# A transform and a mixture of experts in one kernel: stage one beside the making of the matrices, turned matrices by products, and stages and logits that lag

## Chip, cores, metric

One core of one Trainium2 chip. The metric is the device time of one execution in microseconds (us), median of several. Runs here fell on several chips, and the same kernel takes 13 to 14% longer on some than on another, so times are compared on one chip only, and across chips by their ratio to the kernel before on the same chip.

## The reference

Eight images of 2496 rows and 256 channels. Each is filtered in the frequency domain, then every row goes to the one expert of eight that a gate with a bias per modality picks.

```python
def _attn_ref(x, filt_r, filt_i):                      # x (8, 2496, 256)
    X = np.fft.rfft(x, axis=1)
    Y = X * (filt_r + 1j * filt_i)[None, :, :]
    return np.fft.irfft(Y, n=x.shape[1], axis=1).astype(np.float32)

def _moe_ref(x, modality_id, w_gate, modality_bias, w1, w2):   # x (19968, 256), 8 experts, F 1024
    logits = x @ w_gate + modality_bias[modality_id]
    e_idx = np.argmax(logits, axis=1)
    # ... gate_w: softmax probability of the chosen expert
    for e in range(E):
        mask = e_idx == e
        h = np.maximum(x[mask] @ w1[e], 0.0)
        out[mask] = gate_w[mask, None] * (h @ w2[e])
```

## The kernel before

The transform is done by products in three stages. Stage one (L392) multiplies x with `w1m` and writes its result to memory (`b1_d`). Stage two reads it back with other rows on the partitions (`t2`), multiplies with `w2m` (L411), with the filters, and with the turned matrices `a1m` and `a2m` (L418, L419), and writes (`b2_d`). Stage three reads that back (`t4`) and multiplies with `wbm` (L462, L463); its rows `yo` are transposed (L472) and multiplied with the gate (L477). Then the image is routed, its rows are scattered into bins, and blocks of 256 rows of one expert go through two products (L645, L657). All matrices are made on the chip.

One pass of the inner loop is called a slot: a piece of every stage and 2.25 steps of expert work (a quarter of a block's products each).

```python
    bp = ctx.enter_context(tc.tile_pool(name="fbig", bufs=3))      # t2 and t4 together
    # ...  a1m, a2m: transpose w2m, then scatter the columns while copying out of PSUM
        for src, dst in ((w2m, a1m), (w2x, a2m)):
            for s0 in range(0, NS, SPB):
                tp = tpp.tile([KB, SPB, P], BF16, tag="tp")
                for i in range(SPB):
                    nc.tensor.transpose(tp[:, i, :KB], src[:, s0 + i, :], ident[:KB, :KB])
                nc.vector.tensor_copy(
                    dst[:, s0:s0 + SPB, :].rearrange("p s (jr t) -> p s t jr", jr=4),
                    tp[:, :, :KB].rearrange("p s (t jr) -> p s t jr", jr=4))
    # ...
    def stage2(g, k):
        s = k * EV
        if s < NS:
            if s % SCH == 0:                                       # load and use in one slot
                # ...
                nc.sync.dma_start(st[g]["t2"], src[:, s:s + SCH, :])
    # ...  stage3: the previous piece is transposed, copied and multiplied in one slot
            nc.tensor.transpose(pT[:, i, dc, :], yo[:, ub + i, dc * P:(dc + 1) * P], ident)
            # ...
            nc.vector.tensor_copy(yT, pT)
            # ...
            nc.tensor.matmul(psL[:, i, :], lhsT=yT[:, i, dc, :], rhs=wg[:, dc, :], ...)
    # ...  the main loop
    for i in range(B + 4):
        for k in range(NP + 1):                                    # 14 slots to an image
            if i < B and k < NP:
                stage1(i, k)
            if 0 <= i - 1 < B and k <= NS // EV:
                stage2(i - 1, k)
            if 0 <= i - 2 < B and k <= NPY:
                stage3(i - 2, k)
            # ...  scatter to bins, padding
            if 0 <= i - 2 < B and k == NPY + 1:
                route(i - 2)
                # ...
            owed += STEPS                                          # 2.25
            while owed >= 1:
                owed -= 1
                moe.step()
```

## Time and profile before

| | before |
|---|---|
| time, median of 3 | 946.2 us (942.0 to 947.9) |
| span of the profiled run | 935.8 us |
| first stage-one, stage-two, stage-three product | 43.5, 72.1, 127.1 us |
| last stage-three product | 712.2 us |
| from there to the end | 223.6 us |

The page's first part, busy us and share of the span by engine, shows that no engine is full:

```profile
PE 654.5 (70%) x4886; PEld 491.7 (53%) x4886; DVE 410.6 (44%) x1249; ACT 385.0 (41%) x689; POOL 375.6 (40%) x423
```

So the time is read by stretches, not by engines. The five times in the table are seams: start, filling of the three stages, steady work, and the expert work that is left. How each stretch looked before is shown in the prediction.

### The profile page before, as it was taken

The numbers are of one execution on the slowest core, as the hardware profiler recorded it, in microseconds if no ns is written. First come the engines' busy times: TensorE is split into PE (matmuls) and PEld (weight loads), VectorE is DVE, ScalarE is ACT, GpSimd is POOL, SyncE is SP. The second block draws the span as 40 slices with busy tenths as digits, with TensorE's granted clock in tenths as the row PEclk, the third lists the DMA queues.
The fourth block names the chain that finished last, engine by engine and source line by source line (L and its number), as shares of the span: only waits on it lengthen the run. The fifth ranks groups of instructions, "written<-read, shape, count | busy, mean of one in ns | idle before, by whom it ended". The sixth has DMA issues, their size and how long they took to land.

```text
span 935.8 us, 15940 instructions
## 1 busy us (share of the span) xinstructions
PE 654.5 (70%) x4886; PEld 491.7 (53%) x4886; DVE 410.6 (44%) x1249; ACT 385.0 (41%) x689; POOL 375.6 (40%) x423
## 2 busy tenths in 40 slices
PE   0316359459359776858877786779588449999996
PEld 0205236336236554645664565557356338878775
DVE  8812124424524543643472345447335324444442
ACT  1024334335235443634553463436133225555553
POOL 7032100450540543354444335343553664444545
PEclk9999999999656887978996898789788789999999
DMA  9299974644635742564563435232322323323320
GB/s 142 40 194 209 212 145 114 142 117 99 154 95 128 162 118 80 121 168 112 135 157 101 123 101 142 83 106 71 117 67 64 98 90 98 102 88 103 92 75 1
DMA packets 94347, 106.80 MB, mean 114 GB/s; under 512 B 13163, under 2 KB 77457, under 8 KB 94163
## 3 DMA queue, kind: packets, MB, share of 16 engines
q0 software_dynamic: 31008, 52.03, 25.1%
q1 hardware_dynamic: 63258, 53.75, 22.7%
q8 instruction: 44, 0.72, 0.3%
q14 instruction: 37, 0.29, 0.1%
HBM read 74.43 MB, written 54.31 MB: 138 GB/s over the span
## 4 chain that ended last, share of the span: by engine, by line
PE 55%; DMA 10%; issue 10%; another core or an unknown queue 9%; DVE 9%; ACT 6%; POOL 0%; DVEq 0%; POOLq 0%; SPq 0%; ACTq 0%
PE hps L645 16%; PE ops L657 16%; DMA b_d<-t 5%; PE ps L463 4%; PE ps L462 4%; PE lt L472 3%; DMA t<-b_d 3%; ACT t L395 3%; PE pz L418 3%; PE pz L419 2%; PE ps L392 2%; PE pT L634 2%; PE ps L411 2%; ACT hT L649 2%
## 5 line engine op out<-in xcount | busy, mean ns | idle before, releaser
L649 ACT ACTIVATE hT<-hps 128x512 f16<-128x512 f32 x340 | 198.6, 597 | 279.1 <-PE hps L645 139.6
L667 POOL DMA_INDIRECT out_dram<-osb,meta x170 | 167.7, 987 | 272.8 <-DVE osb L664 223.5
L645 PE MATMUL hps<-xT,w 128*128 128x256 f16 x1360 | 232.5, 291 | 32.8 <-issue 17.9
L657 PE MATMUL ops<-w2sb,hT 128*128 x1360 | 228.4, 288 | 10.8 <-issue 9.6
L534 POOL DMA_INDIRECT bins_d<-yo,pos_i x160 | 156.7, 979 | 50.9 <-issue 48.6
L645 PEld LDWEIGHTS <-w 128*128 128x128 f16 x1360 | 131.1, 103 | 62.4 <-issue 40.0
L657 PEld LDWEIGHTS <-hT 128*128 128x128 f16 x1360 | 138.6, 103 | 45.2 <-issue 19.1
L395 ACT CAST t<-ps 96x512 f16<-96x512 f32 x104 | 59.7, 582 | 125.5 <-PE ps L392 54.8
L425 DVE TENSOR_TENSOR p<-xf,g 104x512 f16<-104x512 f16 x96 | 40.7, 424 | 144.1 <-ACT xf L423 135.5
L411 PE MATMUL ps<-t,w2m 104*104 104x256 f16 x192 | 49.0, 348 | 78.4 <-DMA t<-b_d 54.3
L137 POOL DMA_DIRECT2D xt<-in_x_dram x32 | 17.6, 549 | 214.6 <-PE ps L392 175.7
L624 DVE COPY w<-w1sb 128x2048 f16 x85 | 59.2, 697 | 65.8 <-PE ops L657 40.9
L462 PE MATMUL ps<-t,wbm 96*96 96x256 f16 x160 | 58.7, 367 | 36.0 <-ACT t L395 17.9
L664 DVE TENSOR_SCALAR osb<-ops,meta 128x256 f32<-128x256 f32 x170 | 75.3, 477 | 16.3 <-PE ops L657 6.0
L418 PE MATMUL pz<-p,a1m 104*104 104x256 f16 x192 | 61.3, 334 | 23.4 <-DVE p L425 7.0
L423 ACT CAST xf<-ps 104x512 f16<-104x512 f32 x96 | 56.3, 588 | 51.1 <-PE ps L411 40.3
L411 PEld LDWEIGHTS <-w2m 104*104 104x104 f16 x192 | 29.6, 164 | 83.5 <-DMA t<-b_d 55.6
L432 ACT CAST z<-pz 104x512 f16<-104x512 f32 x96 | 56.6, 590 | 38.3 <-PE pz L419 13.5
L635 DVE COPY xT<-pT 128x512 f16<-128x512 f16 x85 | 35.8, 421 | 79.6 <-PE pT L634 36.2
L392 PE MATMUL ps<-xt,w1m 96*96 96x256 f16 x208 | 53.5, 356 | 16.2 <-ACT t L395 15.9
L419 PE MATMUL pz<-xf,a2m 104*104 104x256 f16 x192 | 62.5, 340 | 0.3
L474 DVE COPY yT<-lt 128x512 f16<-128x512 f16 x80 | 33.7, 421 | 62.4 <-PE lt L472 45.8
(188 smaller groups left out, 667.7 us busy)
## 6 DMA issues: line engine op xcount, KB each, us to landing
xs<-bins_d SPq DMA_DIRECT2D x85, 130.0 KB
t<-b_d SPq DMA_DIRECT2D x24, 416.0 KB
b_d<-z SPq DMA_DIRECT2D x48, 208.0 KB
xt<-in_x_dram POOLq DMA_DIRECT2D x24, 384.0 KB
b_d<-t SPq DMA_DIRECT2D x48, 192.0 KB
t<-b_d SPq DMA_DIRECT2D x24, 384.0 KB
w1sb<-in_moe_w_dram POOLq DMA_DIRECT2D x8, 512.0 KB
w2sb<-in_moe_w_dram POOLq DMA_DIRECT2D x8, 512.0 KB
```

What stands on the lines that cost most here:

```text
L392: nc.tensor.matmul(ps[:KA, i, :], lhsT=w1m, rhs=xt[:, t - t0 + i, :], start=True, stop=True)
L395: nc.scalar.copy(st[g]["t1"][:, k % 2], ps[:KA])
L411: nc.tensor.matmul(ps[:KB, i, :], lhsT=w2m[:, s + i, :], rhs=st[g]["t2"][:, s % SCH + i, :], start=True, stop=True)
L418: nc.tensor.matmul(pz[:KB, i, :], lhsT=a1m[:, s_ + i, :], rhs=p1[:, i, :], start=True, stop=False)
L419: nc.tensor.matmul(pz[:KB, i, :], lhsT=a2m[:, s_ + i, :], rhs=p2[:, i, :], start=False, stop=True)
L462: nc.tensor.matmul(ps[:KA, i, :], lhsT=wbm, rhs=t4[:, t - t0, :], start=True, stop=True)
L534: ins = nc.gpsimd.indirect_dma_start(out=bins_d[:, :], out_offset=IOA(ap=st[g]["pos"][:rows, t:t + 1], axis=0), in_=st[g]["yw"][:rows, t, ...
L645: mm = nc.tensor.matmul(hps[:, k, :], lhsT=b["w1"][:, dc, ft * P:(ft + 1) * P], rhs=b["xT"][:, dc].rearrange("p i t -> p (i t)"), start=(d ...
L649: nc.scalar.activation(b["hT"][:, q * FQ:(q + 1) * FQ, :], hps, AF.Relu)
L657: nc.tensor.matmul(b["ops"][:, i, :], lhsT=b["hT"][:, ft, i * P:(i + 1) * P], rhs=w2sb[:, ds(b["ej"], 1), ft, :], start=(ft == 0 and i == ...
L664: nc.vector.tensor_scalar_mul(osb[:, i, :], b["ops"][:, i, :], gate[:, i, :])
L667: ins = nc.gpsimd.indirect_dma_start(out=out[:, :], out_offset=IOA(ap=b["meta"][:, i, 0:1], axis=0), in_=osb[:, i, :], in_offset=None, **kw)
```

## The change

Four parts, meant to shorten the start and to keep PE fed in the middle.

1. *Start.* Stage one of the first image is issued as soon as `w1m` exists; the other matrices come after it in the program. The turned matrices are made by a product with a permuted identity, so that the copies out of PSUM are contiguous and can be split between DVE and ACT. Two smaller things ride along: the filters are read from memory once and copied, not read twice, and the experts' weights are asked for from the first slot of the loop on.
2. *Slots between stages and loads ahead.* Three slots lie between the end of one stage of an image and the start of the next, where there was one; the loads of `t2` and `t4` are issued two slots before their use. Their three shared buffers stay three.
3. *Logits.* A piece's transposition comes one slot after it, its gate products two slots after.
4. *Routing* is split in two slots (count, place) and comes later.

The diff, cut to its core (the moved lines that make room for it are left out):

```diff
+    for k in range(NP):
+        input_piece(0, k)                    # stage one of image 0, before the other matrices
...
+    perm = gen.tile([KB, KB], BF16, name="perm")
+    nc.vector.tensor_copy(perm.rearrange("p (jr t) -> p t jr", jr=4),
+                          ident[:KB, :KB].rearrange("p (t jr) -> p t jr", jr=4))
+    SPB = 4
+    for s0 in range(0, NS, SPB):
+        for src, dst in ((w2m, a1m), (w2x, a2m)):
+            tp = pp.tile([P, EV * D], F32, tag="ps", name="tp")
+            for i in range(SPB):
+                nc.tensor.matmul(tp[:KB, i * KB:(i + 1) * KB], lhsT=src[:, s0 + i, :], rhs=perm,
+                                 start=True, stop=True)
+            ev = nc.vector.tensor_copy if dst is a1m else nc.scalar.copy
+            ev(dst[:, s0:s0 + SPB, :].rearrange("p s c -> p (s c)"), tp[:KB, 0:SPB * KB])
...
-                nc.tensor.transpose(tp[:, i, :KB], src[:, s0 + i, :], ident[:KB, :KB])
-                nc.vector.tensor_copy(
-                    dst[:, s0:s0 + SPB, :].rearrange("p s (jr t) -> p s t jr", jr=4),
-                    tp[:, :, :KB].rearrange("p s (t jr) -> p s t jr", jr=4))
...
+        ub, uc = u0 - EV, u0 - 2 * EV
+        if 0 < k <= NPY:                     # transpose piece k-1
...
+        if k > 1:                            # gate products of piece k-2
+            yT = st[g]["yT"]
...
+    GAP = NP + 1
+    OFF2 = NP + 3
+    OFF3 = OFF2 + NS // EV + 1 + 3
+    LEAD = 2
+    n = NP
+    while True:
+        for g in range(1, B):
+            if 0 <= n - g * GAP < NP:
+                input_piece(g, n - g * GAP)
+        for g in range(B):
+            k = n - g * GAP - OFF2
+            if (k + LEAD) % 4 == 0 and 0 <= k + LEAD < NS // EV:
+                load_t2(g, (k + LEAD) // 4)
+            if 0 <= k <= NS // EV:
+                stage2(g, k)
+        for g in range(B):
+            k = n - g * GAP - OFF3
+            if (k + LEAD) % 3 == 0 and 0 <= k + LEAD < NPY:
+                load_t4(g, (k + LEAD) // 3)
+            if 0 <= k <= NPY + 1:
+                stage3(g, k)
+            if k == NPY + 2:
+                count(g)
+            if k == NPY + 3:
+                place(g)
```

In the changed kernel L222 is stage one, L431 to L439 stage two, L477 and L478 stage three, L489 the transposition, L494 the gate products, L672 and L684 the expert products.

## The prediction

> **What bounds the kernel now.** The whole is no single engine's time: the page gives PE 70% busy, DVE 44%, ACT 41%, POOL 40%. The work is cut into slots: one slot is one pass of the inner loop, a piece of each stage and 2.25 steps of expert work, and 14 slots make an image. So I cut the span at events found in the timeline of PE: first stage-one product at 43.5 us, first stage-two product (L411) at 72.1, first stage-three product (L462) at 127.1, the expert products in steady supply from about 290, last stage-three work at 716, pure expert work from 772. The table of windows then says what each stretch lacks. Columns: window, its length, busy us of PE, PEld, DVE, ACT, POOL, granted clock, DMA share, GB/s.
>
> ```profile
> 0.00:43.50 43.50, 5.62 (x50) 5.19 (x51) 38.64 (x84) 4.21 (x4) 18.83 (x39) 1.00 0.69 94
> 43.50:72.10 28.60, 7.09 (x28) 4.90 (x27) 5.02 (x18) 7.37 (x14) 8.44 (x12) 1.00 0.96 180
> 72.10:127.10 55.00, 24.67 (x101) 18.57 (x101) 11.04 (x26) 19.92 (x38) 9.77 (x14) 1.00 1.17 210
> 127.10:290.00 162.90, 112.96 (x606) 75.28 (x607) 63.41 (x216) 62.90 (x112) 47.77 (x54) 0.85 0.51 118
> 290.00:716.00 426.00, 324.79 (x2514) 238.85 (x2513) 198.31 (x654) 189.89 (x346) 181.92 (x193) 0.84 0.44 114
> 772.00:935.80 163.80, 149.46 (x1344) 125.49 (x1342) 73.97 (x183) 85.31 (x149) 76.33 (x78) 0.98 0.27 80
> ```
>
> The reader sees five regimes: DVE alone for 43 us; DMA saturated (share about 1) to 127 us; PE with gaps and a clock of 0.84 to 0.85 to 716; 56 us of last routing (not shown); then PE full at clock 0.98.
>
> The timeline of the first 43 us shows what DVE does: six copies out of PSUM that scatter columns, about 4 us each, with PE waiting for the buffer between them and stage one starting only afterwards.
>
> ```profile
> 20.43 7.51 DVE L272 COPY a1m<-tp 104x832 f16<-104x832 f16 x2
> ...
> 27.56 4.04 DVE L272 COPY a1m<-tp 104x832 f16<-104x832 f16 x1
> ...
> 31.23 11.39 DVE L272 COPY a2m<-tp 104x832 f16<-104x832 f16 x3
> ...
> 43.55 3.30 PE L392 MATMUL ps<-xt,w1m 96*96 96x256 f16 x14 [0.27 <-DVE bias_b L331]
> ```
>
> In the middle, PE's own waits (window 253 to 716 us) are led by stage openings: L411 is the first product on a freshly read t2, L462 on a t4.
>
> ```profile
> PE ps L462 <- ACT t L395: 17.9, 8, 4.1
> PE ps L411 <- issue: 13.1, 3, 4.7
> PE ps L411 <- DMA t<-b_d: 10.8, 2, 10.4
> PE ps L462 <- issue: 9.3, 3, 4.2
> ...
> PE lt L477 <- DVE yT L474: 6.4, 9, 2.2
> PE lt L477 <- issue: 5.3, 6, 3.2
> ```
>
> The name after the arrow is not always the cause. In the timeline the load issued by SP at 404.9 us is what the L411 of 409.6 us waited for, although the row says "issue".
>
> **What the Trainium skill says.** (1) "TensorE: Matmul & The Clock Gate", Part 1, says that after an idle window of about 3.4 us PE falls to half clock and needs as much busy time to come back. The trace agrees in kind: 0.50 in the slice 257 to 281 us, where PE has gaps, 1.00 in the slices from 796 on, where it has none; so a gap costs more than its length. (2) The same page, Part 2, step by step, says that matmuls stay in program order and only weight loads are pulled ahead. The trace agrees: the L411 at 492.15 us came 4.48 us late, and expert products (L645, L657), which need no t2, followed it only then. (3) "DMA: Bandwidth & Descriptors", Issuing engines are not separate DMA queues, says that all transfers share 16 engines. The 1.17 share at 210 GB/s between 72 and 127 us, weights beside stage traffic, agrees. (4) "VectorE: DVE Perf Modes", Mode 1×, has one result per cycle as the fallback (1.04 ns an element at its 0.96 GHz); here the scattering copy took 4.0 us for 832 elements, 4.8 ns each. The measurement decides: that form is far below the page's fallback.
>
> **The change, part by part.**
>
> *The start.* The six scattered copies (20.43 to 42.7 us, 22.3 us of DVE) go. Instead a product with a permuted identity brings the columns in order, and twelve contiguous copies of 104x416 follow, six on ACT, six on DVE. From the row L484 (128x512 f32 to f16, 688 ns) one is about 0.57 us on DVE; from L395 (582 ns) 0.48 us on ACT. So about 3.5 us, the two side by side. Stage one of the first image needs only w1m, ready at 8.8 us, and x, landed by about 12, and now runs from about 12 us beside the rest. Its 13 evictions took 44.2 to 56.8 us before, paced by landing writes; I give them 12 to 26 us. Sine, w2m and the turned matrices then end near 31 us. On SP the copies of g stand ahead of the last write of stage one, so I add 5 us, then a write and a read back (56.8 to 72.1 before; with less beside it, I take 8 us). Stage two starts at 38 (32 to 45) instead of 72.
>
> *The saturated stretch.* Not all 34 us survive. Up to 127 us the DMA moved (from the three windows) 43.5 x 94 + 28.6 x 180 + 55 x 210 = 20.8 MB. The changed order still issues all eight experts' weights in this stretch, and the filters' second read is replaced by copies of equal size. 20.8 MB at 210 GB/s are 99 us, from 4 us on: stage three can start near 105 us. Gain: 22 us.
>
> *Until experts are steady.* From stage three's start to the first full table there are 36 slots before and 37 after (offsets 28 and 64; 32 and 69). Before: 163 us, with idle gaps of 9.6 and 10.4 us at the two openings and six smaller ones of together about 17. With loads two slots ahead and three slots between stages I expect two thirds gone, 25 us, less one slot of 4 us. Gain: 21 us.
>
> *The steady stretch.* It has 84 slots before and after (slot 64 to 148; 56 to 140 of the new loop), so only the time per slot changes: 455 us over 84 is 5.4 us. The four load rows above, and 0.8 us from L462 behind a DMA, sum to 51.9 us. I take 60% off, 31 us, because buffers do not grow: t2 and t4 share three, a load two slots early holds one for six or five slots, and laying the seven loads on 14 slots gives four wanted at once in two places. One t4 load each image must wait there. Lagged logits take away the two L477 rows, 11.7 us; I take 10. Fewer cold phases: 325 us of busy PE at 0.84; at 0.87 it would be 11 us less. Gain: 52 us, leaving 4.8 us a slot.
>
> *The end.* 37 blocks remain after the last table opens, in both. Their pace is PE's, about 4.15 us a block by the chain of waits (L657 at 786.78, 790.87, 795.01 us); the padding and the last scatter (716 to 772) are not touched. Gain: 0.
>
> *Sum.* 935.8 - 22 - 21 - 52 = 841 us in the trace; the times stand about 9 us above the traced run (946.2 against 937.5). Predicted: 850 us, 10% less.
>
> **The rivals.** *The DMA eats the head start.* Weights and x now come earlier, SP's queue can hold writes behind a load that waits for a buffer, and stage two would start early only to wait for its writes. For it: share 1.17 before 127 us. Against it: only 0.27 between 23 and 47 us, room that is now used. It leaves a gain of about 10 at the start and 20 in the middle: about 900 us. *PE or PSUM becomes the bound.* Three ps buffers carry five tiles a slot; the evictions, not loads, may set the slot. For it: ACT behind L395 is among the releasers. Against: ACT is busy 190 of 426 us. Then the steady stretch gains 15 instead of 52: about 887. *Gaps and clock help each other.* If PE never idles 3 us, the clock goes to nearly 1 and a slot to 4.3 us, with 40 us more gained: about 810. For it: pure expert work holds 0.98. Against: the waiting t4 load.
>
> **Range and chances.** The start's gain follows from plain removal (at least 10), the steady stretch has the widest error, 10 to 90 us. Range 805 to 897. Faster by over 2% (below 927): 0.95; within 2%: 0.04, if both pessimistic rivals hold; slower: 0.01.
>
> **What would show it.** First L431 (stage two) near 38 us; first stage-three product near 105; DMA share near 1 from 5 to 100 us; no copy of 4 us on DVE; PE's waits for t2 and t4 reduced by over half and those of the logits near nil; clock over 0.87 in the steady stretch; still about 190 us from the last table to the end. I am wrong if stage three starts after 120 us, or if steady slots stay above 5.2 us, or if the gain comes from the end.

## The result, and the profile after

| | before | after |
|---|---|---|
| time, median of 4 runs on one chip | 944.1 us (936.4 to 947.9) | 875.1 us (872.8 to 879.7) |
| span of the profiled run | 935.8 us | 878.0 us |
| first stage-one, -two, -three product | 43.5, 72.1, 127.1 us | 16.7, 46.1, 100.1 us |
| first product of the second block of experts, last stage-three product | 293.8, 712.2 us | 252.6, 645.4 us |
| from there to the end | 223.6 us | 232.6 us |

The ratio is 0.9285, 95% interval 0.921 to 0.936: faster. A ratio here is the mean time of one kernel's fast runs over that of the other's (in the experiments without the profiled run), so it isn't quite the ratio of the medians quoted. A run counts as slow when it is over 1.5% above the fastest of its kernel.

The table of windows of the changed kernel, cut near its own seams (columns as in the prediction):

```profile
0.00:16.60 16.60, 0.00 (x0) 0.00 (x0) 7.70 (x61) 1.62 (x2) 9.84 (x24) 1.00 0.93 161
16.60:46.10 29.50, 13.59 (x82) 10.79 (x82) 15.81 (x42) 13.98 (x24) 5.28 (x13) 1.00 0.79 166
46.10:100.10 54.00, 27.46 (x116) 21.83 (x116) 12.76 (x30) 23.13 (x44) 14.94 (x21) 0.60 1.17 214
100.10:250.00 149.90, 116.00 (x627) 78.62 (x628) 62.53 (x221) 64.96 (x116) 47.41 (x54) 0.53 0.66 151
250.00:645.40 395.40, 302.42 (x2416) 231.02 (x2414) 187.32 (x627) 179.10 (x326) 178.91 (x188) 0.86 0.43 117
706.00:878.00 172.00, 154.63 (x1352) 127.27 (x1351) 75.42 (x185) 86.32 (x151) 77.11 (x80) 0.96 0.25 77
```

The clocks 0.60 and 0.53 here and the 1.00 and 0.85 of before are not to be compared: the trace of before has no clock record until 232 us, that of the changed kernel none until 54 us, and the view prints 1.00 where there is none. PE was busy 0.185 us a product in the row from 100 us (116.00 us, 627 products) and 0.186 in that from 127 us before (112.96 us, 606).

Seam by seam the 57.8 us between the traces are: 27.0 us until stage three begins, 14.2 us in the filling (until the second block of experts begins: 166.7 to 152.5 us), 25.6 us in the steady stretch (418.4 to 392.8 us), and 9.0 us given back at the end. The steady stretch is the surprise: its clock went only from 0.84 to 0.86, and PE's idle time in it only from 101 to 93 us; the rest is busy time, 317.4 us in 2462 products before and 299.8 us in 2402 after.

The timeline of the start, lines of DVE, PE and ACT picked out (start, length, engine, line, instruction, and in brackets the idle time and what ended it):

```profile
12.71 0.21 DVE L348 CAST mids<-mrawc 32x48 f16<-32x48 int32 x1 [5.28 <-DMA mrawc<-in_moe_modality_id_dram]
...
16.66 3.38 PE L222 MATMUL ps<-xt,w1m 96*96 96x256 f16 x14 [16.66 <-DVE w1m L205]
...
29.15 1.07 ACT L225 CAST t<-ps 96x512 f16<-96x512 f32 x2 [3.16 <-DMA b_d<-t]
30.11 2.38 ACT L190 ACTIVATE w2m<-q,zbias 104x2496 f16<-104x2496 f32 x1
...
33.32 0.56 PE L309 MATMUL tp<-perm,w2m 104*104 104x104 f16 x4 [6.70 <-DVE w2m L293]
...
35.10 0.59 DVE L312 CAST a1m<-tp 104x416 f16<-104x416 f32 x1 [0.24 <-PE tp L309]
...
39.01 1.09 PE L222 MATMUL ps<-xt,w1m 96*96 96x256 f16 x4
...
46.15 0.67 PE L431 MATMUL ps<-t,w2m 104*104 104x256 f16 x2 [5.18 <-DMA t<-b_d]
```

The 4 us copies are gone; one of 416 columns takes 0.59 us. What now holds the start is order: DVE reaches `w1m` only behind a cast of modality ids, whose first reader runs 32 us later (44.6 us); ACT reaches the sine of `w2m` only behind an eviction (a copy out of PSUM) that waits for a landing write; and PE reaches the last three pieces of stage one, at 39.01 us, only behind the turning products, which wait for that sine until 33.32 us.

PE's waits of the changed kernel in the middle (window 215 to 650 us; us in total, times, longest):

```profile
PE ps L477 <- ACT t L225: 18.8, 11, 4.3
PE lt L489 <- ACT xf L443: 16.6, 6, 4.2
PE ps L477 <- issue: 13.2, 4, 4.9
PE ps L431 <- issue: 12.0, 3, 6.9
...
PE lt L494 <- DVE yT L498: 7.1, 5, 3.2
```

Beside the rows of before in the prediction: the row of L411 behind the DMA (10.8 us) is gone, the row of stage three behind ACT's copy of stage one (17.9 us then) is as large as ever, and the transpositions L489 have a wait that they did not have, for a PSUM buffer which ACT empties. Waits changed their owner more than their sum (121 us of such rows before, 108 after).

### The profile page after: what moved, and what is told of

It reads as the page before. It is cut to its first block, busy times and chain, and to the rows that moved or that the text cites. A ratio compares the mean times of both kernels' runs of the same rounds, so it can differ in the third digit from the quotient of the medians.

```text
span 878.0 us, 15948 instructions
## 1 busy us (share of the span) xinstructions
PE 650.8 (74%) x4886; PEld 497.7 (57%) x4886; DVE 385.7 (44%) x1248; ACT 387.3 (44%) x695; POOL 367.7 (42%) x413
## 4 chain that ended last, share of the span: by engine, by line
PE 23%; issue 17%; POOL 8%; another core or an unknown queue 4%; DMA 4%; DVE 3%; ACT 2%; POOLq 0%; SPq 0%; DVEq 0%; ACTq 0%
PE hps L672 7%; PE ops L684 6%; POOL out_dram L694 6%; DMA out_dram<-osb,meta 2%; PE ps L478 2%; POOL bins_d L561 2%; PE ps L477 2%; PE lt L489 1%; DMA bins_d<-yo,pos_i 1%; ACT hT L676 1%; PE ps L431 1%; PE pT L661 1%; PE pz L439 1%; PE pz L438 1%
## 5 line engine op out<-in xcount | busy, mean ns | idle before, releaser
L672 PE MATMUL hps<-xT,w 128*128 128x256 f16 x1360 | 231.4, 293 | 32.8 <-ACT hT L676 16.5
L684 PE MATMUL ops<-w2sb,hT 128*128 x1360 | 226.6, 289 | 9.8 <-issue 9.3
L684 PEld LDWEIGHTS <-hT 128*128 128x128 f16 x1360 | 141.2, 104 | 45.2 <-issue 18.4
L672 PEld LDWEIGHTS <-w 128*128 128x128 f16 x1360 | 131.9, 104 | 61.2 <-issue 24.8
L477 PE MATMUL ps<-t,wbm 96*96 96x256 f16 x160 | 56.8, 355 | 40.4 <-ACT t L225 18.8
L222 PE MATMUL ps<-xt,w1m 96*96 96x256 f16 x208 | 53.3, 358 | 36.0 <-DVE w1m L205 16.7
L431 PE MATMUL ps<-t,w2m 104*104 104x256 f16 x192 | 48.4, 344 | 40.4 <-issue 12.0
L498 DVE COPY yT<-lt 128x512 f16<-128x512 f16 x80 | 33.8, 422 | 94.2 <-remote 43.5
L438 PE MATMUL pz<-p,a1m 104*104 104x256 f16 x192 | 62.4, 338 | 16.1 <-ACT t L225 5.9
L439 PE MATMUL pz<-xf,a2m 104*104 104x256 f16 x192 | 62.9, 341 | 1.3 <-DVE xf L446 1.1
L489 PE MATMUL lt<-ident,yo 128*128 128x128 f16 x320 | 40.2, 264 | 24.4 <-ACT xf L443 16.6
```

The lines of the kernel that those rows point to most:

```text
L431: nc.tensor.matmul(ps[:KB, i, :], lhsT=w2m[:, s + i, :], rhs=st[g]["t2", s // SCH][:, s % SCH + i, :], start=True, stop=True)
L438: nc.tensor.matmul(pz[:KB, i, :], lhsT=a1m[:, s_ + i, :], rhs=p1[:, i, :], start=True, stop=False)
L439: nc.tensor.matmul(pz[:KB, i, :], lhsT=a2m[:, s_ + i, :], rhs=p2[:, i, :], start=False, stop=True)
L477: nc.tensor.matmul(ps[:KA, i, :], lhsT=wbm, rhs=t4[:, t - t0, :], start=True, stop=True)
L672: mm = nc.tensor.matmul(hps[:, k, :], lhsT=b["w1"][:, dc, ft * P:(ft + 1) * P], rhs=b["xT"][:, dc].rearrange("p i t -> p (i t)"), start=(d ...
L684: nc.tensor.matmul(b["ops"][:, i, :], lhsT=b["hT"][:, ft, i * P:(i + 1) * P], rhs=w2sb[:, ds(b["ej"], 1), ft, :], start=(ft == 0 and i == ...
```

## The experiments

Twelve runs of ten kernels, all correct, all made from the changed kernel unless said. The first four fell on one chip (call it C; before 824.5 us), the next four on a second (A; before 940.0 us), the last four on a third (B; before 934.0 us). Times are medians of four runs, but for the one look. Line numbers shift by up to four between variants; L668 in some is L672 of the changed kernel.

### The new start alone

```diff
-    LEAD = 2
+    LEAD = 0
-    OFF2 = NP + 3
-    OFF3 = OFF2 + NS // EV + 1 + 3
+    OFF2 = NP + 1
+    OFF3 = OFF2 + NP + 1
# logits in the slot after their piece, count and place in one slot at k == NPY + 1, as before
```

> The changed kernel with the old loop offsets (14 slots between the stages), loads at the point of use, logits in the same slot and routing in one slot: only the new start is left of the change. Both traces put the whole gain at the first stage-three product at 27 us (127.1 to 100.1). Theory A (the start gives what it gave there, the new loop gives the rest): about 917 us, ratio 0.970. Rival B (the middle is bound elsewhere and the new loop gives next to nothing): about 880 us, ratio 0.935. Rival C (the head start is eaten up when the loop cannot use it): ratio above 0.985.

Measured on chip C: 807.7 us, ratio 0.981 (0.974 to 0.988). Rival B falls. The value lies between theory A and rival C, and the interval reaches C; with the line for "faster" at 2% it is unclear.

### Without the loads ahead

```diff
-    LEAD = 2
+    LEAD = 0
```

> The changed kernel with LEAD 0: t2 and t4 loads are traced where they are used, all else kept. Theory A (loads ahead take the openings' waits away): 15 to 30 us slower than the changed kernel, 890 to 905 us. Rival B (three shared buffers and held-up completions set the slot, the three spare slots already cover the landing): within 6 us of 875.

Measured on chip C: 757.7 us, ratio 0.9161 (0.912 to 0.921). Both theories compare with the changed kernel, which never ran on this chip, so neither can be read from it.

### Logits one piece behind

Transposition, copy and gate products in one slot as before; everything else as in the changed kernel (routing still split and later).

```diff
-        if k > 1:
-            yT = st[g]["yT"]
+        if k > 0:
+            # ... transpose, copy to yT, then the gate products of the same piece
```

> The changed kernel with the logits one piece behind as before (transposes, copy and logits of one piece in one slot), routing in the same slots. Theory A (PE's wait for the copy, 11.7 us in the kernel before, was on the path): 8 to 12 us slower, about 885 us. Rival B (other work filled that wait or another wait takes its place): within 4 us of 875.

Measured on chip C: 764.0 us, ratio 0.926 (0.921 to 0.932). For the same reason it decides between its theories no more. Neither undoing the loads ahead nor undoing the logits' lag brought the time anywhere near that of the start alone.

### Four buffers for the loads

```diff
-    bp = ctx.enter_context(tc.tile_pool(name="fbig", bufs=3))
+    bp = ctx.enter_context(tc.tile_pool(name="fbig", bufs=4))
```

> The changed kernel with four instead of three buffers for t2 and t4. Theory A (one t4 load each image waits for a buffer, as the prediction counted): 10 to 25 us faster, 850 to 865 us, and the waits before the first products on t4 (L477) fall from 32 us in the steady stretch to under 15. Rival B (those waits come from PSUM buffers freed late by ACT): within 5 us of 875, L477 waits as before.

Measured on chip C: 750.0 us, ratio 0.9101 (0.906 to 0.915). It is the fastest of its set, but its nearest neighbour, without the loads ahead, is only 0.7% behind with overlapping intervals, and the changed kernel itself was not in the set. So a worth of the fourth buffer over 1% isn't shown. The waits ahead of L477 (250 to 640 us) are down to 0.2 us, but without the loads ahead, and with three buffers, they were only 8.9 us on this chip.

### The chip matters: the changed kernel and the kernel before again

> The changed kernel itself once more, beside its variants. The first four variants ran on a chip on which the kernel before took 824 us and not 944, and in their traces no wait is put down to another core or an unknown queue (the first chip's traces have 60 us of such waits for ACT's hT alone). Theory A: those hold-ups belong to the first chip; without them the changed kernel is at about 0.92 of before (0.912 to 0.928), the same as without the loads ahead (0.916) and with the logits one piece behind (0.926), and the loads ahead are worth less than 1%. Rival B: the loads ahead do pay where nothing else is in the way; then this run is at 0.895 to 0.908, over 1% below the variant without them. On a chip like the first one (before at about 944 us) it is at 0.92 to 0.936 again.

Measured on chip A: 876.8 us, ratio 0.929 (0.921 to 0.937). That is the first result again, and decides nothing between A and B of the expectation, because the chip was of the slow kind.

> The kernel before, unchanged, for a trace on this chip. Theory: on a chip where it takes about 824 us, the chain up to the first expert product takes as long as in the first trace within 8 us (first stage-two product at about 72 us, first expert product at about 224 us), the waits put down to another core are gone, PE's idle time between 250 and 640 us falls from 102 us to 60 to 85 us, and a stage-two product of L411 takes under 0.30 us in place of 0.319. Rival: everything is slower by the same factor on the first chip; then the first stage-two product comes at 63 us.

Measured on chip A: 931.2 us (one look, so its state is unknown; it is below every other run of before on this chip), and its trace has the late releases too, so this expectation could not be tested either. It serves as the trace of before for the table further down.

What the two kinds of chip do differently shows in one kernel that ran on both, the start alone. Its waits of ACT, over the whole run, on chip B:

```profile
ACT hT L672 <- PE hps L668: 143.3, 193, 3.7
ACT hT L672 <- remote: 50.0, 12, 8.1
```

and its windows from 250 to 500 us, first chip C and then chip B:

```profile
250.00:500.00 250.00, 207.53 (x1724) 157.98 (x1721) 137.49 (x464) 140.03 (x255) 121.11 (x128) 0.91 0.55 141
```

```profile
250.00:500.00 250.00, 183.62 (x1385) 135.47 (x1385) 112.69 (x375) 113.80 (x208) 96.77 (x105) 0.81 0.49 125
```

"remote" means that the trace names no releaser on this core. On chip C no wait of this kernel is put down to it; on B twelve waits of ACT alone lose 50 us. In the first 100 us, where loads set the pace, the two are alike: 36.00 and 36.20 us of busy PE. The span is 805.0 us on C and 909.9 on B. The late releases are not the only difference: the granted clock between 250 and 500 us is 0.91 on C and 0.81 on B, and a product of the experts takes 286 and 302 ns there. Which of the two comes first, and why, is not settled by anything run here.

### Old offsets, logits two pieces behind

```diff
-    LEAD = 2
+    LEAD = 0
-    OFF2 = NP + 3
-    OFF3 = OFF2 + NS // EV + 1 + 3
+    OFF2 = NP + 1
+    OFF3 = OFF2 + NP + 1
```

> The changed kernel with the stages at their old offsets (no slots between one stage and the next) and no loads ahead; the logits stay two pieces behind. The variant with only the new start was at 0.981, the one with the slots between stages but no loads ahead at 0.916. Theory A, it is the slots between the stages that carry the middle: this one is at 0.97 to 0.985, with the idle time of PE ahead of L431 and L477 back at over 20 us between 250 and 640 us, ended by the loads. Rival C, the logits' lag carries it: at 0.91 to 0.93.

Measured on chip A: 875.6 us, ratio 0.932 (0.925 to 0.939). The theory that the slots between stages carry the middle falls: without them and without loads ahead the kernel is as fast as with them (0.929 on the same chip). The value lies just above rival C's range, which its interval overlaps.

### More expert steps in a slot

```diff
-    STEPS = 2.25
+    STEPS = 2.75
```

> The changed kernel with 2.75 steps of expert work to a slot in place of 2.25. Some 37 blocks of expert work are left when the last routing is done and run then with PE over 95% busy; PE has about 58 us of idle time in the steady stretch on the faster chip, of which 24 us lie ahead of expert products. Theory: the steady stretch has the blocks to take (ten blocks come in each 14 slots, 2.86 steps to a slot), idle time is filled, and the time falls by 5 to 20 us, to 0.90 to 0.915 of before. Rival: the added steps only push the stages back, since PE is 88% busy there; then the end is shorter by what the steady stretch gains and the ratio is that of the unchanged one within 0.8%.

Measured on chip A: 864.8 us (862.9 to 866.1), ratio 0.918 (0.912 to 0.925); the changed kernel beside it 876.8 (869.8 to 878.8). The intervals of the ratios overlap, the runs don't. Counted in the traces, 36.0 blocks are left after the last stage-three product in place of 44.75. The end shrinks by 40 us (233.6 to 193.6), the stages end 26 us later (643.4 to 669.9). So most of what is moved only changes place, and the time is some 13 us shorter. It isn't all filled idle time, as the theory had it: over the whole trace PE's idle time fell only from 223.9 to 219.6 us, and its busy time from 653.1 to 643.9 us, at a mean granted clock of 0.804 and 0.822. The ratio lies between the ranges of theory and rival.

### Start alone, with logits' lag, with slots: on one chip

The first two are the kernels of above once more; the third has the new start and the slots between stages, but no loads ahead and the logits one piece behind.

> The new start alone (old offsets, no loads ahead, logits one piece behind, as before), a second time, so that it stands on one chip with the next two. It was at 0.981 on the chip where the kernel before takes 824 us; with the logits two pieces behind and all else the same, the other variant was at 0.932, but on a chip where before takes 940 us. Theory L, the logits' lag (without slots between stages) carries the middle: 0.97 to 0.985 here, whichever chip it is, 30 us or more above that other variant. Rival S, on a chip with held-up releases the whole gain is that of the start: 0.925 to 0.942 on such a chip, within 1% of the full change.

> New start and logits two pieces behind, stages at their old offsets, no loads ahead; a second time, for the comparison on one chip. On a chip where before takes 940 us: 0.925 to 0.94, as it was. On the faster chip: theory L 0.915 to 0.93 (the logits' lag is enough); rival, the slots between stages are needed there: 0.965 to 0.985.

> New start and slots between the stages, no loads ahead, logits one piece behind. Theory L': either lag takes the same wait away, so slots alone are as good as the logits' lag alone: within 1% of the run without slots (0.92 to 0.94). Theory L: only the logits' lag counts; then this one lies with the start alone, at 0.97 to 0.985. Rival S: all three runs of this set are within 1% of each other.

Measured on chip B:

| kernel | time, us | ratio (95%) |
|---|---|---|
| start alone | 910.6 | 0.976 (0.969 to 0.983) |
| start and logits two behind | 864.6 | 0.924 (0.915 to 0.933) |
| start and slots between stages | 875.1 | 0.937 (0.931 to 0.944) |

Theory L' holds best, though the two lags are 1.4% apart and not within 1%: either alone brings most of the middle's gain, and both together with the loads ahead (0.929, but on chip A) bring no more. Rival S falls: the start alone is worth 2.4% here and 1.9% on chip C, both unclear by the 2% line. One of the four runs with the logits' lag was slow and is left out of its ratio.

The seams of the traces, from the timeline of PE (before and full change on chip A, the others on B):

| | first stage three | last stage three | between | from there to the end |
|---|---|---|---|---|
| before | 126.7 | 702.9 | 576 | 226.5 |
| start alone | 103.9 | 690.5 | 587 | 219.3 |
| start and logits' lag | 102.5 | 634.5 | 532 | 227.6 |
| start and slots | 100.8 | 651.4 | 551 | 226.5 |
| the full change | 100.1 | 643.4 | 543 | 233.6 |

The start's gain of 23 to 27 us is there in every variant when stage three begins. Alone, it has shrunk to 12 us when stage three ends and grows again to 20 us at the end; but the two rows are from two chips. By the times on one chip the start alone is 23 us faster on B and 17 us on C, so on B no loss is shown. The lags take 36 to 55 us out of the stretch between (beside the start alone), and not their sum.

The waits of PE between 100 and 500 us suggest why they are substitutes. Before:

```profile
PE ps L411 <- DMA t<-b_d: 49.6, 6, 18.4
PE ps L462 <- ACT t L395: 14.9, 5, 4.3
```

The start alone:

```profile
PE ps L431 <- DMA t<-b_d: 53.1, 7, 17.3
PE pz L438 <- ACT t L225: 14.0, 17, 10.3
```

Start and logits' lag:

```profile
PE ps L431 <- DMA t<-b_d: 30.3, 6, 9.0
PE ps L431 <- DVE yo L504: 12.1, 4, 5.8
PE ps L477 <- ACT t L225: 10.3, 7, 4.2
```

Start and slots:

```profile
PE ps L477 <- ACT t L225: 19.5, 9, 4.3
PE lt L493 <- DVE yT L490: 13.5, 10, 4.9
...
PE lt L488 <- DVE lg L503: 8.7, 2, 5.8
```

The full change:

```profile
PE ps L477 <- ACT t L225: 28.3, 13, 5.2
PE pz L438 <- ACT t L225: 11.0, 10, 8.7
...
PE ps L477 <- DMA t<-b_d: 6.6, 3, 2.5
```

The start leaves the wait for `t2` as it was (49.6 and 53.1 us). The logits' lag takes away 23 us of it. The slots take it all, but then the logits (13.5 and 8.7 us) and PSUM buffers that ACT has not yet emptied (19.5 us) are waited for. With everything in place the loads and the logits are quiet and ACT's copies of stage one hold 28.3 us. Time in which PE ran neither a product nor a weight load, between 100 and 640 us: 147 us before, 147 with the start alone, 117, 122 and 122 for the last three.

One thing stays open. The runs with either lag share a part that the start alone has not: routing in two slots, and later. It was never run by itself, so "the logits' lag" and "the slots" each mean "with the later routing".

### The pieces that paid, together

```diff
-    bp = ctx.enter_context(tc.tile_pool(name="fbig", bufs=3))
+    bp = ctx.enter_context(tc.tile_pool(name="fbig", bufs=4))
-    STEPS = 2.25
+    STEPS = 2.75
-    nc.vector.tensor_scalar_mul(w1v[:, 1, :], w48v, bit0[:KA])
+    w1_done = nc.vector.tensor_scalar_mul(w1v[:, 1, :], w48v, bit0[:KA])
+    with tc.issue_after(w1_done.ins):        # around the casts of the modality ids
```

> The changed kernel with what the runs pointed to: four buffers for the loads of stages two and three (was worth about 1.5% against its like), 2.75 steps of expert work to a slot (1.1%), and stage one's matrix ahead of the casts of the modality ids (first stage-one product at about 10 us in place of 17, first stage-two product 4 to 7 us earlier than 46). If the three add up: 0.885 to 0.905 of before. Rival: buffers and steps fill the same idle time, and the early matrix only meets the loads of the first 100 us; then 0.905 to 0.92.

Measured on chip B: 857.3 us (845.8 to 860.6), ratio 0.912 (0.902 to 0.922). The middle of the interval lies in the rival's range, its lower end in the other: the pieces most likely don't add. Two of the four runs, the profiled one among them, were over 1.5% above the fastest and count as slow, so the ratio rests on two runs, and on one of them, 845.8 us, above all. From the profiled run only the start is read:

```profile
8.31 3.37 PE L222 MATMUL ps<-xt,w1m 96*96 96x256 f16 x14 [8.31 <-DVE w1m L205]
19.48 1.07 PE L222 MATMUL ps<-xt,w1m 96*96 96x256 f16 x4 [7.80 <-ACT t L225]
...
43.74 0.67 PE L432 MATMUL ps<-t,w2m 104*104 104x256 f16 x2 [5.21 <-DMA t<-b_d]
```

Stage one begins 8.4 us sooner than in the changed kernel, then waits 7.8 us for its buffers, and stage two begins only 2.5 us sooner: the early matrix meets the same evictions and writes, and the last pieces of stage one again run only behind the turning products (36.6 us). As a whole it is the fastest kernel on its chip, but its interval touches that of the full change and holds the ratio with 2.75 steps alone (0.918).

## Why the prediction was right or wrong

The direction and the range (805 to 897) were right, the latter also because it gave the steady stretch 10 to 90 us; the size was too large (10% said, 7.2% measured). Of the sum -22, -21, -52, 0, the trace gave -27, -14, -26, +9.

*The start.* The mechanism held: no scattered copies, stage one beside the rest, and then saturated DMA (share 1.17). Stage two was said for 38 us and came at 46.1. Two steps failed. "w1m, ready at 8.8 us": a cast of modality ids, scheduled ahead of it, waited 5.28 us for its load. And "13 evictions ... 12 to 26 us": they took from 17.4 to 42.5 us. When the cast was moved in the last experiment, `w1m` was ready at 8.3 us, but the evictions ran from 9.0 to 40.0 us and stage two gained only 2.5 us of the 8. So the evictions are the larger step: they wait for landing writes, the sine waits behind one of them, the turning products for the sine, and the last three pieces of stage one, on PE, for these. DMA, said to be near its limit from 5 us on, was at a share of 0.79 between 16.6 and 46.1 us, so its rate did not hold stage two. Stage three came at 100.1 and not 105. That fits fewer bytes having moved by then: 16.6 x 161 + 29.5 x 166 + 54.0 x 214 = 19.1 MB, against 20.8 assumed, at nearly the assumed rate.

*The filling.* 21 predicted, 14 measured, and only 5 in the pair of traces on chip A (161.1 to 155.8 us). That the lags bring it is borne out on chip B: 166.6 us with the start alone, 149.3 and 153.4 with one lag.

*The steady stretch* is the mis-sized term: 52 predicted, 26 measured, one slot fewer included. Of its parts:
- "I take 60% off" the 51.9 us of load waits, 31 us. The same kinds of rows after sum to 18.8 + 13.2 + 12.0 = 44.0 us, so 8 us went. The step that failed is to call them all load waits. The semaphore events of the trace before (no view prints them) show a load landing just ahead of the L411 rows and the small row of L462, 13.1 + 10.8 + 0.8 = 24.7 us. In the other two rows of L462, 27.2 us, the load had landed 20 us or more before, or none was waited for: where a releaser is named, it is ACT emptying a PSUM buffer. After, a load landed within 3 us ahead of only one wait, of 1.2 us. So the load waits went almost wholly, more than was said, and the other waits grew by 16 us.
- "Lagged logits take away the two L477 rows", 10 us. The waiting products did become rare (7.1 us for L494), but the transpositions ahead of them now wait for PSUM (16.6 us, L489). On top of the slots the logits' lag is worth at most 1% (0.926 without it, 0.916 with it and without the loads ahead, on chip C), and the slots are worth nothing on top of the logits' lag (0.932 without them, 0.929 with them and the loads ahead, on chip A): each covers for the other.
- "Fewer cold phases", 11 us: the clock rose to 0.86, not 0.87. PE's busy time per product fell from 0.129 to 0.125 us, over 2402 products about 10 us by my estimate, so this part was about right.

The slot was said to fall from 5.4 to 4.8 us. Counted between the seams it fell from 418 us over 71 slots, 5.9 us, to 393 us over 70, 5.6 us. Over the prediction's own 84 slots, which end with the last scatter (768.0 and 706.3 us in the traces), it fell from 5.6 to 5.4 us; its 455 us for them were 19 us short. Either count crosses the line that I had set for being wrong ("above 5.2 us").

*The end.* 0 predicted, +9 measured. 44.75 blocks are left after the last stage-three product in place of 44.25 (counted in L672), half a block or 2 us. Of the other 7 us, 5 lie between the last stage-three product and the last scatter: 55.9 us before, 61.0 after (57.5 and 62.4 on chip A). That fits the later routing: on chip B the start alone, with routing as before, has 51.6 us there, the variants with one lag 59.3 and 57.5. The end is no constant: with 2.75 steps in a slot it is 40 us shorter.

*The rivals.* The middle is nearest to the second one, "PE or PSUM becomes the bound", in its PSUM half: it gave 15 us to the steady stretch and 887 us in all, and 26 us and 875 were measured. Its argument against itself, that ACT is busy under half of the time, was no argument: ACT's copies come late not because ACT is full but because they wait themselves: in the full change on chip A, between 100 and 500 us, these copies of stage one waited 31.8 us for late releases and 29.3 us for PE. On chip C, where no release is late, the row "PE ps L477 <- ACT t" is 0.2 us in the variant without loads ahead, between 260 and 500 us: there PSUM is no such bound. (The full change was not run on that chip.) The first rival, that loads eat the head start, was wrong: stage three began 27 us earlier. The third, that the clock goes to nearly 1, did not occur (0.86).

## What to carry to other kernels

Two changes that relieve the same chain need not add: run each alone and both, on one chip, before giving each its share (here "both" ran only on another chip). Before a wait is priced, see from the semaphores what it waits for, and then what stands directly behind it in the same buffers and the same in-order engine; here load, logits and PSUM waits took each other's place. And read a head start at the end of the run, not at its first seam.

## What the Trainium skill lacked or had wrong

- "VectorE: DVE Perf Modes", Mode 1×, takes odd strides and PSUM operands at the fallback rate of one result per cycle. Here the copy out of PSUM that scatters columns took 4.0 us for 832 elements, 4.8 ns each; the contiguous one took 0.59 us for 416 f32 elements, 1.4 ns each with its fixed part. (The type in PSUM changed with the order, so the scatter's share alone isn't shown.) "SBUF — State Buffer", Door 1, does say that an access which crosses to a new 16-byte line pays a penalty; the trace agrees in kind, but I found no figure for a strided DVE copy on either page.
- No page that I know of says that chips differ: one and the same kernel (the start alone) had a span of 805.0 us on one chip and 909.9 us on another, and before took 824.5, 934.0 and 940.0 us on three. Ratios differed less: 0.981 and 0.976 for that kernel.
- No page that I know of speaks of releases that reach an engine late with no releaser named: 50.0 us in 12 waits of one kind of ACT's instructions on chip B, none on chip C. Their cause is open, and the granted clock differs between the two as well (0.81 and 0.91).
- "TensorE: Matmul & The Clock Gate", Part 1, was borne out on the drop at gaps (0.50 in the slice from 257 to 281 us before). It warns, under Seeing it yourself, that the trace's events of the clock gate have been seen to be unreliable; the form met here is that they can be missing at the start. Between 50 and 100 us the variant with early logits is told 1.00 and the one without loads ahead 0.56, with 24.97 us in 104 products and 24.59 us in 105; the first has no clock record before 188 us, the other has one from 53 us on. An early 1.00 in a table of windows is no reading, in the prediction's first rows either.
